# Long convolution and gated MLP in one kernel: matrices made ahead on GpSimd, conversions loaded from ScalarE's queue, tables copied

## The chip, the core and the metric

The kernel runs on one core of a Trainium2 chip. The core has TensorE (PE in the profile; its weight loads are PEld), VectorE (DVE), ScalarE (ACT), GpSimd (POOL) and SyncE (SP). Each takes its own instructions in a fixed order and waits at an instruction until what it needs is there. Transfers are issued by an engine's queue, in the kernel before by SP's alone, and run beside the engines. The metric is the device time of one execution in microseconds (us); of several executions the median counts.

## What is computed

```python
# attention block: batch 4, S = 12480, D = 128, filter order 64
h_filt = (np.maximum(pos_emb @ w1, 0.0) @ w2) * np.exp(-0.01 * pos)[:, None]
u = x * v
Uf = np.fft.rfft(u, n=2 * S, axis=1)
Hf = np.fft.rfft(h_filt, n=2 * S, axis=0)
y = np.fft.irfft(Uf * Hf[None], n=2 * S, axis=1)[:, :S, :]
x = (x * y).reshape(4 * S, D)
# mlp block: 128 -> 2048 -> 128
h = x @ w_in
out = ((h * np.cos(h)) @ w_out).astype(np.float32)
```

So a long convolution of `x*v` with a filter that is itself computed, a product with `x`, and an MLP with the activation h·cos(h). `moe_w_in` and `moe_w_out` arrive as float64.

## The kernel before

**The transform.** The convolution is done by a transform of length 2·96·120 that is split in two steps, N1 = 96 and N2 = 120, each a set of matrix products in float32. Rows of the sequence are taken in pairs (row and mirrored row), and their sums and differences are what the first step takes in. A batch entry goes through first step (`f1_units`, 64 units, one per pair of channels), second step (48 units, one per pair of frequencies k1), product with the filter's transform, and two inverse steps (`i1_units`, 64 units, and `i2_units`, 30 groups). The filter's transform is made once, together with the first batch entry's (`f2_both_units`), and stored in DRAM as `hd`; the matrices of the second step are stored as `wd`, and later batch entries load both.

**The order of the work.** It is written out by hand. `units` is a generator of the steps of one stage; the loops at the end of the kernel advance several such generators in turn, and every engine gets its instructions in the order in which Python emits them. Before 313 us the stages follow each other as this:

1. 0 to 26 us: the filter's MLP (`filter_turn`, `filter_hidden`). POOL computes angles for the sine tables (`Tables.sines`), ACT turns them into sines (`Tables.finish`, L227).
2. 26 to 52 us: `filter_out` (L371), 30 passes; between them `first_u` advances, the products and sums of x and v of the first batch entry (`u_multiply` L411, `u_sums` L421). Their loads (L394) come in through five places for pairs of rows, three pairs ahead. `ALONE` says from which pair on POOL takes a part.
3. 52 to 115 us: first step of the filter (L429; evicted by L448 and L450, four units of five by ACT, one by DVE). `first_u` goes on every second half-unit.
4. 115 to 156 us: first step of the first batch entry (L429, evicted by L441).
5. 156 to 256 us: second step of filter and batch entry together. For each pair `before` makes two matrices w (`make_w`: ACT writes a term into a bank of PSUM, L302, DVE adds the rest, L304) and stores them (L642); PE multiplies (L462, L465 for the filter, L135 for the batch entry); ACT copies the filter's part out as h (L653), which is stored (L655) and multiplied by DVE (L478) and summed by POOL (L485).
6. 256 to 312 us: first inverse step (L135 with `cs`), with `some_groups` making a part of the last step's tables beside it.

After that comes the main loop: the MLP's tiles, with the other convolution steps in between.

**The conversions.** `moe_w_in` and `moe_w_out` are turned from float64 words into float32 in 16 pieces of 128x256 during stages 3 and 4 (`convert_units`, `float32_store`): one load of 256 KB (L181), five DVE operations (L147 to L155), two on ACT (L160, L162), two on POOL (L163, L165), one store (L166). Loads run three pieces ahead through three buffers. One call of the generator is made every tenth half-unit from number 50 on; the first call only loads.

**The tables.** `inverse_tables` makes three tables with POOL and ACT, `cs` (120x2x120), `rows` (96x4x104) and `tw_t` (96x2x120). They lie in places that later stages overwrite, so they are stored in DRAM (L935) and loaded again: `cs` after stage 3/4's loop into a pool of its own (L953), the others after the second step (L965).

**Memory that is used twice.** The conversions' pool is given up when the last piece is done, and the pool of the second step (`both`: w, t, h) takes its place. Its first w is emitted eight half-units after the end of the conversions, still within the first step of the batch entry.

**PSUM.** Eight banks go round (`bank`). A half-filled order of evictions on ACT or DVE therefore stops PE after at most eight units.

Of the kernel before, what the change touches and what calls it, by code (L numbers as in the profile page):

```python
# [10 lines left out]
F32 = mybir.dt.float32  # L11
I32 = mybir.dt.int32
U32 = mybir.dt.uint32
AF = mybir.ActivationFunctionType
ALU = mybir.AluOpType
# [3 lines left out]
P = 128  # L19
# [15 lines left out]
def kernel(  # L35
# [46 lines left out]
    nc = tc.nc  # L82
# [4 lines left out]
    N1, N2 = 96, 120  # L87
# [3 lines left out]
    H = N2 // 2  # L91
# [18 lines left out]
    LAG = 7  # L110
    ALONE = 7
    WCOL = 256
# [28 lines left out]

    def float32_store(pool, dst, raw, factor):
        lo, hi = raw[:, :, 0], raw[:, :, 1]
# [14 lines left out]

        high = sig[:, :].bitcast(F32)
        nc.scalar.activation(high, sig[:, :], AF.Copy, scale=factor * 2.0 ** -20)  # L160
        low = pool.tile([P, WCOL], F32, name="low", bufs=1)
        nc.scalar.activation(low[:, :], lo, AF.Copy, scale=factor * 2.0 ** -52)  # L162
        nc.gpsimd.tensor_tensor(high, high, low[:, :], op=ALU.add)  # L163
        there = power[:, :].bitcast(F32)
        nc.gpsimd.tensor_tensor(there, high, there, op=ALU.mult)  # L165
        nc.sync.dma_start(dst, there)  # L166

# [7 lines left out]
    def convert_units(pool):  # L175

        raws = []
        for i, (dst, _, factor) in enumerate(pieces):
            while len(raws) < min(i + 3, len(pieces)):
                raws.append(pool.tile([P, WCOL, 2], U32, name="raw", bufs=3))  # L180
                nc.sync.dma_start(raws[-1][:, :, :], pieces[len(raws) - 1][1])  # L181
            yield
            float32_store(pool, dst, raws[i], factor)

# [69 lines left out]
    def inverse_tables(pool):  # L254

        t = Tables(pool, nc.gpsimd)
        part = t.whole([P, 1], [[1, 1]], channel_multiplier=1, name="part")
        part4 = t.whole([P, 1], [[1, 1]], base=1, channel_multiplier=4, name="part4")
        step = t.whole([P, P], [[1, P]], name="step")
        mid = t.whole([P, P], [[1, P]], base=-MID, name="mid")  # L260
        cs, (rows, tw_t) = third_table(pool), last_tables(pool)
        t.sines(step, part, N2, [(cs[:, 0, 0:H + 1], 1), (cs[:, 1, 0:H + 1], 0)],
                eighths=slice(0, H + 1, H))
        t.sines(step[:, 1:H], part, N2, [(cs[:, 0, H + 1:], 0), (cs[:, 1, H + 1:], 1)])
        t.sines(step, part4, 4 * N1, [(rows[:, i, :], q) for i, q in enumerate((0, 1, 2, 3))])
        t.sines(mid, part4, TURN, [(tw_t[:, 0, :], 1), (tw_t[:, 1, :], 0)],
                eighths=slice(H - 1, N2, H))
        return t, ((csd, cs), (rowsd, rows), (twd, tw_t))

# [12 lines left out]

    def third_table(pool):

        return pool.tile([N2, 2, N2], F32, name="cs")

# [23 lines left out]
    def make_w(w, k1, **how):  # L310


        turn(w, even[:, 0, :], even[:, 1, :], tw_w[:, 0, k1:k1 + 1], tw_w[:, 1, k1:k1 + 1],
             **how)

    def make_t(t, n2, copies=(), **how):
# [316 lines left out]
    def f2_both_units(bank):  # L633

        with tc.tile_pool(name="both", bufs=2) as pool:
            ws = {}

            def before(j):
                ws[j] = pool.tile([KE, 2, N2], F32, name="w")
                for i in range(2):  # L640
                    make_w(ws[j][:, i, :], 2 * j + i, half=bank)
                nc.sync.dma_start(wd[j, :, :, :], ws[j][:, :, :])  # L642

            def mm(j, ps, i):
                if i == 0:
                    ps = bank(), bank()
                for k in range(2):
                    f2_mm(ps[1 - i], ws[j], 2 * j, k, filt=i == 0)
                return ps

# [211 lines left out]
    with tc.manual_schedule():  # L862
        with tc.tile_pool(name="psum", bufs=8, space=PSUM) as psum, \
# [13 lines left out]
            with tc.tile_pool(name="layers", bufs=1, side="right") as pool:  # L877
# [26 lines left out]
                sines = forward_tables(pool)  # L904
                last_sines, made_tables = inverse_tables(between)
                peTs = {}
# [21 lines left out]
            for j in range(H // 2):  # L928
                filter_out(bank, aT, ftile, j, w2_sb)
                if j and j % 2 == 0:  # L930
                    last_sines.finish()
                for _ in range(1 + j % 2):
                    next(first_u)
            for kept, here in made_tables:
                nc.sync.dma_start(kept[:, :, :], here)  # L935
            keep.__exit__(None, None, None)
# [7 lines left out]
            with tc.tile_pool(name="convert", bufs=1) as pool:  # L944
                convert = convert_units(pool)
                for i, _ in enumerate(f1):
                    if i % 2 == 0:
                        next(first_u, None)
                    if i >= 50 and i % 10 == 0 and next(convert, True):
                        break  # L950
            lpool = ctx.enter_context(tc.tile_pool(name="late", bufs=1))
            cs = third_table(lpool)
            nc.sync.dma_start(cs[:, :, :], csd[:, :, :])  # L953
            f2 = f2_both_units(bank)
# [18 lines left out]
            with tc.tile_pool(name="ready", bufs=1) as pool:  # L973
                other = some_groups(pool)
                for i, _ in enumerate(i1_units(bank, lambda b: b % 8 == 3)):
                    if i % 4 == 0:
                        next(other, None)
# [110 lines left out]
```

## Time and profile before

| | us |
|---|---|
| three executions | 3684.23, 3684.69, 3687.74; median 3684.69 |
| profiled execution | 3686.0, its span 3684.2 |
| PE busy | 3609.0, 98% of the span |
| DVE, ACT, POOL busy | 2820.9, 2228.0, 2750.0 |
| granted clock of PE, mean | 0.997 |
| filter_out (L371), first to last | 25.9 to 51.6 |
| first step, filter (L429) | 52.5 to 114.7 |
| first step, batch entry (L429) | 114.8 to 156.3 |
| second step (L462, L465) | 156.5 to 251.9 |
| first inverse step | 256.2 to 310.4 |

How to read it: "busy" counts the time in which an engine had an instruction running. A row such as `L304 DVE ... w<-even,tw_w,ps 124x120 x2 [0.24 <-DMA wd<-w]` names the line, the engine, what is written from what, how many instructions were merged, and how long the engine stood idle before it and for whom. Records of PE matmuls are two for each matmul of float32. Instructions that issue transfers stand under their queue, SPq.

### The profile page before, as it was taken

What the parts mean: (1) busy time and instruction counts of PE and PEld (TensorE: products, weight loads), DVE (VectorE), ACT (ScalarE), POOL (GpSimd) and SP (SyncE); (2) the same over time, 40 slices, a digit from 0 to 9 for tenths busy, and PEclk for the clock granted to TensorE, in tenths of its full rate; (3) what the DMA queues carried; (4) which work ended last, traced back from release to release, by engine and by line L of the source; (5) the groups of instructions that cost most, each with busy time, mean ns of one, the idle gap of its engine ahead of it and who ended that gap; (6) DMA issues with size and microseconds to landing.
All of it is one profiled execution on the core that took longest, in us unless ns stands there. A gap on an engine that the chain in (4) does not pass through costs nothing.

```text
span 3684.2 us, 101739 instructions
## 1 busy us (share of the span) xinstructions
PE 3609.0 (98%) x40810; PEld 2552.8 (69%) x40810; DVE 2820.9 (77%) x5313; ACT 2228.0 (60%) x4474; POOL 2750.0 (75%) x3240
## 2 busy tenths in 40 slices
PE   7999999999999999999999999999999999999999
PEld 6777777766668776666667776766667786666666
DVE  6887886688887776688887777578887667777777
ACT  5666666665554556656555556665555446666666
POOL 7466996588874886588874887578884448878877
PEclk9999999999999999999999999999999999999999
DMA  6354541022213651022211662012220360000000
GB/s 183 113 174 124 160 144 31 18 70 70 70 48 85 171 157 29 18 70 67 74 41 32 174 167 75 13 53 70 71 69 16 88 170 22 19 23 20 19 25 14
DMA packets 226032, 281.78 MB, mean 76 GB/s; under 512 B 18883, under 2 KB 163067, under 8 KB 225435
## 3 DMA queue, kind: packets, MB, share of 16 engines
q1 hardware_dynamic: 225563, 275.29, 26.6%
q8 instruction: 324, 5.31, 0.6%
q14 instruction: 145, 1.19, 0.1%
HBM read 194.75 MB, written 80.46 MB: 75 GB/s over the span
## 4 chain that ended last, share of the span: by engine, by line
PE 83%; DVE 4%; POOL 2%; ACT 1%; issue 1%; DMA 0%; SPq 0%; ACTq 0%; POOLq 0%; DVEq 0%
PE ph L135 30%; PE cv L135 17%; PE accb L814 17%; PE acca L814 13%; PE cv L429 3%; PE cv L139 1%; DVE gt L789 1%; DVE gt L783 1%; PE ph L139 1%; ACT gt L782 1%; POOL ts L797 0%; POOL slots L421 0%; POOL ts L800 0%; ACT tile L845 0%; DVE xt L411 0%
## 5 line engine op out<-in xcount | busy, mean ns | idle before, releaser
L782 ACT ACTIVATE gt<-ph 128x512 int32<-128x512 f32 (+1 forms) x1380 | 823.1, 596 | 1147.0 <-PE ph L135 1087.4
L783 DVE SCALAR_TENSOR_TENSOR gt<-ph,gt 128x512 f32<-128x512 f32 (+1 forms) x1380 | 948.9, 688 | 717.1 <-ACT gt L782 714.1
L797 POOL TENSOR_TENSOR ts<-gt 128x512 f32<-128x512 f32 (+2 forms) x784 | 1006.5, 1284 | 582.5 <-PE accb L814 551.1
L135 PE MATMUL ph<-at,w_in_sb 128*64 128x512 f32 (+1 forms) x5520 | 1426.4, 592 | 13.5 <-ACT tile L845 6.5
L788 ACT ACTIVATE gt<-gt 128x512 f32<-128x512 f32 (+1 forms) x1568 | 971.8, 620 | 3.8 <-DVE gt L783 3.2
L789 DVE TENSOR_TENSOR gt<-ph,gt 128x512 f32<-128x512 f32 (+1 forms) x1380 | 936.0, 678 | 0.0
L814 PE MATMUL accb<-ts,w_out_sb 128*64 128x128 f32 (+2 forms) x9408 | 650.5, 272 | 0.0
L801 POOL TENSOR_TENSOR ts<-gt,ts 128x256 f32<-128x256 f32 (+2 forms) x784 | 575.6, 734 | 61.5
L800 POOL TENSOR_TENSOR ts<-ts,gt 128x256 f32<-128x256 f32 (+2 forms) x784 | 574.6, 733 | 61.5
L814 PEld LDWEIGHTS acca<-gt,w_out_sb 128*64 128x64 f32 x6272 | 398.5, 137 | 267.8 <-issue 231.5
L814 PEld LDWEIGHTS accb<-ts,w_out_sb 128*64 128x64 f32 x9408 | 544.2, 137 | 0.0
L814 PE MATMUL acca<-gt,w_out_sb 128*64 128x128 f32 (+2 forms) x6272 | 479.1, 272 | 0.0
L814 PEld LDWEIGHTS accb<-gt,w_out_sb 128*64 128x64 f32 x3136 | 225.1, 137 | 255.0 <-issue 198.7
L135 PEld LDWEIGHTS ph<-at,w_in_sb 128*64 128x64 f32 x5520 | 353.4, 137 | 33.3 <-ACT tile L845 14.7
L485 POOL TENSOR_TENSOR slots<-slots,t 120x256 f32<-120x256 f32 x383 | 281.1, 740 | 125.9 <-DVE t L484 68.4
L135 PEld LDWEIGHTS cv<-slots,tm 96*64 96x64 f32 (+1 forms) x3840 | 242.7, 126 | 120.2 <-issue 116.0
L814 PE MATMUL accb<-gt,w_out_sb 128*64 128x128 f32 (+1 forms) x3136 | 311.5, 273 | 4.8 <-DVE ot L835 3.2
L814 PE MATMUL acca<-ts,w_out_sb 128*64 128x128 f32 (+1 forms) x3136 | 308.4, 272 | 1.5 <-POOL ts L800 1.2
L135 PE MATMUL cv<-slots,tm 96*64 96x128 f32 (+1 forms) x3840 | 274.1, 285 | 3.9 <-DVE slots L507 3.4
L135 PEld LDWEIGHTS cv<-cs,slots 120*64 120x64 f32 (+1 forms) x3072 | 168.0, 125 | 61.1 <-issue 59.2
L814 PEld LDWEIGHTS acca<-ts,w_out_sb 128*64 128x64 f32 x3136 | 201.2, 137 | 3.0 <-POOL ts L800 2.7
L135 PE MATMUL cv<-slots,w 124*56 124x256 f32 (+1 forms) x1152 | 190.9, 406 | 1.9 <-ACT at L771 1.9
(136 smaller groups left out, 3742.9 us busy)
## 6 DMA issues: line engine op xcount, KB each, us to landing
h<-hd SPq DMA_DIRECT2D x144, 240.0 KB
tm<-td SPq DMA_DIRECT2D x96, 312.0 KB
xs<-in_x_dram SPq DMA_DIRECT2D x120, 208.0 KB
zd<-xs SPq DMA_DIRECT2D x119, 208.0 KB
tile<-zd SPq DMA_DIRECT2D x96, 256.0 KB
xt<-in_x_dram SPq DMA_DIRECT2D x90, 208.0 KB
vt<-in_v_dram SPq DMA_DIRECT2D x90, 208.0 KB
w<-wd SPq DMA_DIRECT2D x144, 116.2 KB
```

The lines of the kernel that those rows point to most:

```text
L135: nc.tensor.matmul(dst[lo:hi], left[:, lo:hi], right, start=start, stop=stop)
L139: nc.tensor.transpose(dst, src, ident[0:n, 0:n])
L429: nc.tensor.matmul(dst[lo:hi], u[:, b, lo:hi, i], c1[0:u.shape[0], r:r + 2, :].rearrange("p r k -> p (r k)"), start=True, stop=True)
L485: (engine if r else nc.gpsimd).tensor_tensor(y[:, r], y[:, r], t[:, r], op=op)
L782: nc.scalar.activation(turns, ph[:, 0:m], AF.Identity, bias=phase)
L783: nc.vector.scalar_tensor_tensor(out=part, in0=ph[:, 0:m], scalar=phase, in1=turns, op0=ALU.add, op1=ALU.subtract)
L788: nc.scalar.activation(part, part, AF.Sin, scale=scale)
L789: nc.vector.tensor_tensor(part, ph, part, op=ALU.mult)
L797: nc.gpsimd.tensor_tensor(ts[:, 0:2, 0:half], gt[:, :, half:2 * half], gt[:, 0, 0:2 * half].rearrange("p (h n) -> p h n", h=2), op=ALU.sub ...
L800: nc.gpsimd.tensor_tensor(t[2], t[1], b11, op=ALU.add)
L801: nc.gpsimd.tensor_tensor(t[3], b21, t[2], op=ALU.subtract)
L814: nc.tensor.matmul(acc[h * CB:(h + 1) * CB, place, 0:r], w_out_sb[:, pair, weight, :], right[:, h * r:(h + 1) * r], start=(pair == 0 and i ...
```

## The change

- *Tables.* The part of `cs` beyond its 61st column is no longer computed: it is copied from the other half when `cs` is stored. The third and fourth row table are the negated first and second, made by ACT. Six angle tables remain of ten; they are taken every third pass of `filter_out` instead of every second. All are stored by `store_tables` after the last pass. `cs` is loaded back into the memory of `even`, when the last matrix has been made from it.
- *Conversions.* The loads are issued from ACT's queue, at first two and then one piece ahead; the low part is written over its source; the store of a piece is issued a call later. Calls start at half-unit 40.
- *Matrices.* `early_matrices` makes the two matrices of every fourth pair (3, 7, ... 47: 24 matrices) on POOL during stages 3 and 4, from half-unit 30 on, every eighth, and stores them to `wd`. In the second step these pairs have no w; their matrices are loaded, each when the early pair before it has been multiplied.
- `ALONE` is 8 instead of 7; the side work of the first inverse step starts at half-unit 14 and comes twice in seven half-units instead of once in four.

```diff
-    ALONE = 7
+    ALONE = 8
+    EARLY = 4
@@ float32_store is now float32_made
-        high = sig[:, :].bitcast(F32)
+        high, low = sig[:, :].bitcast(F32), lo.bitcast(F32)
         nc.scalar.activation(high, sig[:, :], AF.Copy, scale=factor * 2.0 ** -20)
-        low = pool.tile([P, WCOL], F32, name="low", bufs=1)
-        nc.scalar.activation(low[:, :], lo, AF.Copy, scale=factor * 2.0 ** -52)
-        nc.gpsimd.tensor_tensor(high, high, low[:, :], op=ALU.add)
+        nc.scalar.activation(low, lo, AF.Copy, scale=factor * 2.0 ** -52)
+        nc.gpsimd.tensor_tensor(high, high, low, op=ALU.add)
...
-        nc.sync.dma_start(dst, there)
+        return lambda: nc.sync.dma_start(dst, there)
@@ convert_units
-        raws = []
+        raws, store = [], lambda: None
         for i, (dst, _, factor) in enumerate(pieces):
-            while len(raws) < min(i + 3, len(pieces)):
+            while len(raws) < min(i + 2, len(pieces)):
                 raws.append(pool.tile([P, WCOL, 2], U32, name="raw", bufs=3))
-                nc.sync.dma_start(raws[-1][:, :, :], pieces[len(raws) - 1][1])
+                nc.scalar.dma_start(raws[-1][:, :, :], pieces[len(raws) - 1][1])
+                if i:
+                    break
+            if i == 0:
+                yield
+            store()
+            store = float32_made(pool, dst, raws[i], factor)
             yield
-            float32_store(pool, dst, raws[i], factor)
+        store()
@@ inverse_tables
-        t.sines(step[:, 1:H], part, N2, [(cs[:, 0, H + 1:], 0), (cs[:, 1, H + 1:], 1)])
-        t.sines(step, part4, 4 * N1, [(rows[:, i, :], q) for i, q in enumerate((0, 1, 2, 3))])
+        t.sines(step, part4, 4 * N1, [(rows[:, i, :], i) for i in range(2)])
...
+        def store():
+            for i in range(2):
+                nc.scalar.activation(rows[:, 2 + i, :], rows[:, i, :], AF.Copy, scale=-1.0)
+                nc.sync.dma_start(csd[:, i, 0:H + 1], cs[:, i, 0:H + 1])
+                nc.sync.dma_start(csd[:, i, H + 1:], cs[:, 1 - i, 1:H])
+            for kept, made in ((rowsd, rows), (twd, tw_t)):
+                nc.sync.dma_start(kept[:, :, :], made)
@@ new
+    cs = even[0:N2]
+    def early_matrices(pool):
+        for j in range(EARLY - 1, N1 // 2, EARLY):
+            for i in range(2):
+                k1 = 2 * j + i
+                w = pool.tile([KE, N2], F32, name="made", bufs=3)
+                term = pool.tile([KE, N2], F32, name="term", bufs=1)
+                for h, dst in enumerate((w, term)):
+                    nc.gpsimd.tensor_scalar(out=dst[:, :], in0=even[:, h, :],
+                                            scalar1=tw_w[:, h, k1:k1 + 1], scalar2=None,
+                                            op0=ALU.mult)
+                nc.gpsimd.tensor_tensor(w[:, :], w[:, :], term[:, :], op=ALU.add)
+                yield
+                nc.sync.dma_start(wd[j, :, i, :], w[:, :])
@@ f2_both_units
             def before(j):
+                if j % EARLY == EARLY - 1:
+                    if j == EARLY - 1:
+                        load_early(j)
+                    return
...
+                if j == N1 // 2 - 2:
+                    nc.sync.dma_start(cs[:, :, :], csd[:, :, :])
+            def load_early(j):
+                if j < N1 // 2:
+                    ws[j] = pool.tile([KE, 2, N2], F32, name="early", bufs=1)
+                    nc.sync.dma_start(ws[j][:, :, :], wd[j, :, :, :])
...
+                if i and j % EARLY == EARLY - 1:
+                    load_early(j + EARLY)
@@ the loops
-                if j and j % 2 == 0:
+                if j and j % 3 == 0:
                     last_sines.finish()
...
-            for kept, here in made_tables:
-                nc.sync.dma_start(kept[:, :, :], here)
+            store_tables()
...
-                convert = convert_units(pool)
+                convert, matrices = convert_units(pool), early_matrices(pool)
                 for i, _ in enumerate(f1):
                     if i % 2 == 0:
                         next(first_u, None)
-                    if i >= 50 and i % 10 == 0 and next(convert, True):
+                    if i >= 24 and i % 8 == 6:
+                        next(matrices, None)
+                    if i >= 40 and i % 10 == 0 and next(convert, True):
                         break
-            lpool = ctx.enter_context(tc.tile_pool(name="late", bufs=1))
-            cs = third_table(lpool)
-            nc.sync.dma_start(cs[:, :, :], csd[:, :, :])
+                for _ in matrices:
+                    pass
...
-                    if i % 4 == 0:
+                    if i > 10 and i % 7 in (0, 3):
                         next(other, None)
```

More of the change, by code (lines that the diff above doesn't have):

```diff
@@ L139, in transpose, with float32_made @@
         nc.tensor.transpose(dst, src, ident[0:n, 0:n])
-    def float32_store(pool, dst, raw, factor):
+    def float32_made(pool, dst, raw, factor):
         lo, hi = raw[:, :, 0], raw[:, :, 1]
@@ L260, in inverse_tables @@
         mid = t.whole([P, P], [[1, P]], base=-MID, name="mid")
-        cs, (rows, tw_t) = third_table(pool), last_tables(pool)
+        cs = pool.tile([N2, 2, N2], F32, name="cs")
+        rows, tw_t = last_tables(pool)
         t.sines(step, part, N2, [(cs[:, 0, 0:H + 1], 1), (cs[:, 1, 0:H + 1], 0)],
                 eighths=slice(0, H + 1, H))
-        t.sines(step[:, 1:H], part, N2, [(cs[:, 0, H + 1:], 0), (cs[:, 1, H + 1:], 1)])
-        t.sines(step, part4, 4 * N1, [(rows[:, i, :], q) for i, q in enumerate((0, 1, 2, 3))])
+        t.sines(step, part4, 4 * N1, [(rows[:, i, :], i) for i in range(2)])
         t.sines(mid, part4, TURN, [(tw_t[:, 0, :], 1), (tw_t[:, 1, :], 0)],
                 eighths=slice(H - 1, N2, H))
-        return t, ((csd, cs), (rowsd, rows), (twd, tw_t))
+        def store():
[5 more added lines that the diff above has]
+                nc.sync.dma_start(kept[:, :, :], made)
+        return t, store
     class Between:
@@ L281, in tile @@
             return rows if len(shape) == 3 else rows[:, 0]
-    def third_table(pool):
-        return pool.tile([N2, 2, N2], F32, name="cs")
+    cs = even[0:N2]
     def last_tables(pool):
@@ L904 @@
                 sines = forward_tables(pool)
-                last_sines, made_tables = inverse_tables(between)
+                last_sines, store_tables = inverse_tables(between)
                 peTs = {}
```

## The prediction

> **What bounds the kernel now.** I read the page's engine rows first, then busy time by stretches of 10 us over the first 340 us, the waits of two stages, and the timeline at three places.
>
> ```profile
> PE 3609.0 (98%) x40810; PEld 2552.8 (69%) x40810; DVE 2820.9 (77%) x5313; ACT 2228.0 (60%) x4474; POOL 2750.0 (75%) x3240
> ```
>
> PE is busy for 98% of the span, so a gain can only come from where it isn't. The instructions that the diff touches all run before 313 us; after that the program is the same, and every microsecond won or lost before arrives at the end unchanged. The stretches (us from:to, length, busy us and instructions of PE, PEld, DVE, ACT, POOL, then clock, DMA share, GB/s):
>
> ```profile
> 60.00:70.00 10.00, 9.95 (x120) 9.65 (x120) 6.59 (x17) 5.93 (x22) 5.49 (x7) 1.00 0.70 195
> 70.00:80.00 10.00, 8.60 (x101) 7.96 (x102) 7.17 (x18) 3.25 (x12) 5.91 (x8) 1.00 0.73 212
> 80.00:90.00 10.00, 3.47 (x30) 2.49 (x28) 3.71 (x10) 2.49 (x10) 2.73 (x4) 0.79 0.79 223
> 90.00:100.00 10.00, 8.31 (x84) 6.37 (x82) 9.07 (x23) 4.97 (x20) 6.28 (x9) 0.84 0.47 126
> 100.00:110.00 10.00, 8.42 (x66) 6.01 (x64) 8.35 (x22) 5.17 (x22) 7.56 (x10) 0.68 0.28 75
> 170.00:180.00 10.00, 9.93 (x42) 6.75 (x41) 8.85 (x21) 5.91 (x15) 7.03 (x11) 1.00 0.60 181
> ```
>
> Two places are loose. The filter's first step (L429, 52.5 to 114.7) has 512 matmul records; at the 12 per us of the first row they need 42.7 us and take 62.2. The waits of 52 to 115 us (total, times, longest) say why:
>
> ```profile
> ACT sig L160 <- DVE sig L147: 21.6, 6, 10.5
> PE ps L429 <- ACT slots L450: 9.8, 3, 6.5
> DVE sig L147 <- DMA raw<-in_moe_w_in_dram: 7.0, 1, 7.0
> ```
>
> The first conversion's load arrives late, DVE stands on it, ACT behind DVE, PE behind both. The second place is the filter's second step (156.5 to 252), where PE looks full but its weight loads aren't (6.75 of 10). One pair of matrices there:
>
> ```profile
> 178.80 0.59 DVE L304 SCALAR_TENSOR_TENSOR w<-even,tw_w,ps 124x120 f32<-124x120 f32 x2 [0.24 <-DMA wd<-w]
> 179.31 0.69 DVE L478 TENSOR_TENSOR slots<-ps,h 120x512 f32<-120x512 f32 x1
> 179.42 0.24 SPq L642 DMA_DIRECT2D wd<-w  x1
> 179.91 0.68 DVE L478 TENSOR_TENSOR t<-ps,h 120x512 f32<-120x512 f32 x1
> 181.21 0.72 PEld L462 LDWEIGHTS ps<-ftile,w 124*120 124x120 f32 x4 [0.42 <-DVE w L304]
> ```
>
> The next w starts at 180.81, so the period is 2.02 us: 1.80 of DVE work and 0.22 for a buffer that its store still reads. PE waits 0.42 per pair for DVE: DVE is the bound.
>
> A third row fixes when that step may start:
>
> ```profile
> 146.02 0.59 DVE L304 SCALAR_TENSOR_TENSOR w<-even,tw_w,ps 124x120 f32<-124x120 f32 x2 [1.82 <-DMA woutd<-power]
> ```
>
> The step's first w reuses the conversions' memory, so it waits until they are over: GpSimd's (POOL's) last operation of them ended at 143.53, w started 2.5 us later. DVE stands meanwhile, and PE can go on only until its eight banks are used. From w there remain 0.6 us and 13 units of 0.65 (41.7 us over 64): 9.1 us, to 155.1; the step began at 156.5. PE has 1.4 us to spare.
>
> **The change part by part.** *Tables.* 18 POOL operations go (25.55 to 29.92 and 36.20 to 40.56): 8.7 us. DVE waited 9.5 us for POOL at 47, so products of x and v move forward by as much. Four Sin of 0.28 us go, two ScalarE negations come; three stores on SP become six (+0.6 us of issue), behind the negations at about 53 where SP now passes at 60. PE is at its full rate from 26 to 70, so this is worth nothing by itself. ALONE 8 moves one pair (0.73 and 0.97 us) from POOL to DVE, while DVE stood idle: nothing.
>
> *Loads.* 16 issues move from SP to ACT's queue, 0.37 us each (SP's row) or 0.93 (three took 2.78): 6 to 15 us of ACT, which is busy 2.5 to 6 of 10 there; hidden. What stands behind a held load on ACT are evictions, which PE waits for after eight banks, some 5 us. The first two are issued 10 half-units (of 0.37 us) ahead of their use, at about 67.4; landing took 3.0 us from the last of three issues and 5.8 from the first, I take 4.1: 71.5. From there DVE and ACT took 1.15 us and POOL's two operations 1.9 (86.18 to 89.26): the first conversion ends near 75, not 89. So the 7 us wait goes, and PE's idle time at 78 to 106 with it. It isn't won: what is late next is POOL.
>
> The Trainium skill (DMA: Bandwidth & Descriptors, Issuing engines are not separate DMA queues) says that transfers of all issuing engines interleave on the same DMA engines, so another queue saves issue time alone. By it the landing would be the longer 5.8 us and the sum 1.7 us later; no row here shows two queues at once.
>
> *Matrices.* 24 times two tensor_scalar and one tensor_tensor of 124x120 on POOL. Rows of that shape, of the first 50 us:
>
> ```profile
> L204 POOL TENSOR_SCALAR prod<-step,odd_p 124x120 f32<-124x120 f32 x1 | 0.6, 587 | 0.0
> L221 POOL TENSOR_TENSOR turned<-moved,turned 124x120 f32<-124x120 f32 x2 | 0.9, 439 | 0.2
> ```
>
> With the gaps of the timeline (0.69 from one to the next, 0.5 for the last) 1.88 us. Beside DVE work the same shapes took 0.96 and 0.82: 2.74 at worst. In the built order POOL still has, after the first conversion, 21 matrices (39.5), 15 conversions of two 0.73 us (22.5 with gaps) and 7 halves, 4 sums and a memset of x times v (9.9): 71.9 us without a pause, from 75 to 146.9. The last matrix's store must land too, 2.5 us: first w at 149.4, not 146.0. Less the 1.4 to spare, the second step starts 2.0 us later. With clean prices throughout (1.82 and 1.46) it is +0.1; with contended ones (2.2 and 1.87 each, 11 for the rest) POOL ends at 160.3 and it is +15.4. I stay near the clean end because of this pair:
>
> ```profile
> 119.63 0.73 POOL L163 TENSOR_TENSOR sig<-sig,low 128x256 f32<-128x256 f32 x1 [1.14 <-DVE power L153]
> 119.65 0.99 DVE L155 SCALAR_TENSOR_TENSOR power<-raw,power 128x256 uint32<-128x256 uint32 x1
> ```
>
> DVE's operation, 0.43 us alone, ended 0.28 after POOL's: they don't run at once, and DVE paid.
>
> The Trainium skill (SBUF — State Buffer, Who interferes with whom) names this: VectorE's tensor_scalar, or two inputs from SBUF, and GpSimd share a port pair as an exclusive lock, and who starts second waits. The trace agrees (0.99 against 0.43). Counted fully against POOL, that rule gives the contended end.
>
> SP's 24 matrix stores (0.24 each) are past SP's row loads, which run three pairs ahead; the loads no longer bind once POOL does.
>
> *Second step.* In 12 of 48 pairs ACT's two terms, DVE's w and its store go; a load of equal size comes, issued four pairs ahead (some 7 us against 3.4 of landing). Such a pair costs DVE 1.21, the others 1.80: 6.61 for four, PE's weight loads 4 times 1.61 = 6.44. One w in four still follows two pairs after the w whose buffer it takes (store issued 179.42, next use 3.4 later) with only 3.0 us of DVE work between: +0.4. So 7.05 for four instead of 8.08: 12 times 1.03 = 12.4 won, less 1.6 for the first such load, issued one pair ahead only: −10.8 (bounds −16, no wait; 0, below). The cosine table's reload lies under the last pairs; if it landed late, 2 to 3 us.
>
> *Third step* (256 to 310): PE's weight loads are full (10.0 of 10). Its side work starts 14 half-units later at a denser rhythm and reaches the same unit last (112): nothing.
>
> **Sum.** +2.0 − 10.8 = −8.8. The profiled execution took 3686.0 (span 3684.2 and 1.8 around it), 1.3 above the median: 3677.2 for it, 3675.9 against the median 3684.7. I say 3676. About 0.2%, 7.4 us, is what a measurement of this kernel can tell from no change: below 3677.3 or above 3692.1.
>
> **Rivals.** (a) *POOL's queue becomes the bound*: the contended prices, first w at 162.8 or later. For it: matrices are placed just where DVE's conversions run. Against: rows of 107 to 143, where POOL's operations stayed at 0.73. +15.4 − 10.8 = 3689; at 2.74 per matrix POOL ends near 171.5 and it is 3700. Slower than before from 2.30 us per matrix on (the rest as in the forecast: the queue then ends at 155.7). (b) *The second step is bound by transfers*: 356 KB per pair in 2.02 us are 176 GB/s, and the bytes stay. Then only the +2 is left, 3687. Against: DMA share 0.60 there, 0.70 at 195 GB/s earlier. (c) *No cost in the first step and no wait for stores*: −16 + 0.1, 3669. (d) *The loads don't come earlier*, ACT being held by what its issue waits for: first conversion at 89 as now, POOL's end 14 us later; 3690, priced like (a).
>
> **Numbers.** Forecast 0.50 (own range 3671 to 3682: 0.37 faster, 0.13 same); (a) with (d) 0.20 (slower 0.13, same 0.07); (b) 0.15, same; (c) 0.15, faster. Faster 0.52, same 0.35, slower 0.13. Range 3668 to 3691: it takes in (b), (c) and the near end of (a), and leaves out 0.15.
>
> **What will show it.** Right: wait for raw below 2 us; PE's idle time moves from 78–106 to just before the first w, at about 149; POOL busy nearly without a pause from 75 on, tensor_scalar of the matrices at 0.6 to 0.7; four pairs of the second step in 7.05 us, weight loads near 9 of 10. Wrong: POOL rows near 1 us, or pairs still at 2.02 us with waits for hd or wd.

## The result, and the profile after

The changed kernel is slower by 0.3%: 3697.4 us (median of 7 executions, 3696.0 to 3700.5) against 3686.5 (7, 3683.9 to 3690.3), a ratio of 1.0031 with a 95% interval of 1.0019 to 1.0042. The forecast was 3676 with a range up to 3691, and both its sign and its range were missed. The profiled execution took 3697.4, its span 3695.4; that of the kernel before 3686.0 and 3684.2.

The page's engine row of the changed kernel (busy us, share, instructions):

```profile
PE 3607.3 (98%) x40810; PEld 2558.0 (69%) x40810; DVE 2811.3 (76%) x5291; ACT 2215.1 (60%) x4448; POOL 2783.9 (75%) x3293
```

PE has the same work and the span is 11.2 us longer, so PE waited longer. The first start of each stage's matmuls, us, says where:

| | before | after | difference |
|---|---|---|---|
| first step, filter | 52.5 | 52.1 | -0.4 |
| first step, batch entry | 114.8 | 111.3 | -3.5 |
| second step | 156.5 | 164.2 | +7.7 |
| first inverse step | 256.2 | 267.4 | +11.2 |
| second inverse step | 312.2 | 324.3 | +12.1 |

Two places lost: the batch entry's part of the first step (52.9 us instead of 41.7) and the second step, which took 103.2 us to the start of the next instead of 99.7, where the forecast had counted on 10.8 us less. Busy time by stretches, the changed kernel (columns as in the prediction):

```profile
60.00:70.00 10.00, 10.00 (x126) 10.00 (x124) 6.15 (x16) 5.76 (x22) 8.68 (x13) 1.00 0.77 226
70.00:80.00 10.00, 7.11 (x85) 6.44 (x82) 8.99 (x21) 4.98 (x20) 9.08 (x13) 1.00 0.76 216
80.00:90.00 10.00, 7.28 (x66) 5.80 (x63) 5.22 (x13) 2.49 (x10) 9.60 (x14) 0.76 0.65 188
90.00:100.00 10.00, 5.77 (x56) 4.13 (x52) 6.43 (x17) 2.49 (x10) 9.68 (x14) 0.84 0.27 85
140.00:150.00 10.00, 6.18 (x77) 5.07 (x72) 2.02 (x5) 5.43 (x14) 9.43 (x17) 1.00 0.20 63
150.00:160.00 10.00, 6.87 (x62) 5.42 (x64) 2.43 (x6) 1.92 (x4) 0.44 (x1) 0.66 0.08 21
170.00:180.00 10.00, 7.25 (x26) 5.78 (x27) 4.58 (x10) 2.62 (x7) 3.92 (x6) 0.83 0.41 115
200.00:210.00 10.00, 9.69 (x44) 7.44 (x43) 8.62 (x19) 5.53 (x14) 7.08 (x10) 1.00 0.60 180
```

The fifth pair, POOL, is 8.7 to 9.7 of 10 from 60 on and stops at 150. PE still idles between 70 and 100, and again at 140 to 160. Who waited, changed kernel, 52 to 115 us (total, times, longest):

```profile
ACT sig L161 <- DVE sig L148: 22.3, 6, 6.1
DVE slots L449 <- POOL slots L439: 9.8, 6, 2.5
PE ps L457 <- ACT slots L478: 8.4, 3, 5.1
```

The 7 us wait for `raw` is gone, but DVE now waits for POOL's row products, which stand behind matrices in POOL's order; ACT waits for DVE, PE for ACT's evictions. The chain is the old one with another head. The end of POOL's queue, by the timeline:

```profile
150.00 0.44 POOL L340 TENSOR_TENSOR made<-made,term 124x120 f32<-124x120 f32 x1
152.73 0.59 DVE L317 SCALAR_TENSOR_TENSOR w<-even,tw_w,ps 124x120 f32<-124x120 f32 x2 [9.85 <-DMA wd<-made]
153.13 1.22 PE L457 MATMUL ps<-c,slots 104*64 104x192 f32 x6 [6.95 <-DVE w L317]
```

The first w of the second step came at 152.73 instead of 146.02, behind POOL's last matrix and its store, and PE, with all banks full, stood 6.95 us. POOL's rows from 55 to 152 us (busy, mean ns | idle before):

```profile
L337 POOL TENSOR_SCALAR made<-even,tw_w 124x120 f32<-124x120 f32 x24 | 17.7, 737 | 0.0
L337 POOL TENSOR_SCALAR term<-even,tw_w 124x120 f32<-124x120 f32 x24 | 16.7, 694 | 0.0
L163 POOL TENSOR_TENSOR sig<-sig,raw 128x256 f32<-128x256 f32 x16 | 12.3, 766 | 0.1
L340 POOL TENSOR_TENSOR made<-made,term 124x120 f32<-124x120 f32 x24 | 12.0, 498 | 2.0
```

A matrix costs 0.74 + 0.69 + 0.50 = 1.93 us, close to the 1.88 of the forecast. A stretch of the second step, where three pairs with w and one with an early tile (a pair whose matrices are loaded) take turns:

```profile
201.64 0.58 ACT L694 ACTIVATE h<-ps 120x512 f32<-120x512 f32 x1
203.23 0.24 SPq L674 DMA_DIRECT2D wd<-w  x1
203.56 0.84 SPq L696 DMA_DIRECT2D hd<-h  x2
206.38 0.60 ACT L694 ACTIVATE h<-ps 120x512 f32<-120x512 f32 x1 [2.06 <-DMA hd<-h]
207.01 0.69 DVE L506 TENSOR_TENSOR slots<-ps,h 120x512 f32<-120x512 f32 x1 [0.68 <-ACT h L694]
```

Where DVE had less to do, ACT waited 2.06 us for a buffer of h that its store still held, and DVE waited for ACT. Early loads were issued every 8.01 us (191.17 to 255.24, eight periods): four pairs took 8.01 us, against 4 times 2.02 before and 7.05 in the forecast. ACT waited 35.0 us for `hd<-h` in 24 waits; before it was 34.6 us in 43.

### The profile page after: what moved, and what is told of

Read it like the earlier page. It is cut to its first block, busy times and chain, and to the rows that moved or that the text cites. A ratio compares the mean times of both kernels' runs of the same rounds, so it can differ in the third digit from the quotient of the medians.

```text
span 3695.4 us, 101778 instructions
## 1 busy us (share of the span) xinstructions
PE 3607.3 (98%) x40810; PEld 2558.0 (69%) x40810; DVE 2811.3 (76%) x5291; ACT 2215.1 (60%) x4448; POOL 2783.9 (75%) x3293
## 4 chain that ended last, share of the span: by engine, by line
PE 84%; DVE 4%; POOL 1%; ACT 1%; issue 1%; DMA 0%; SPq 0%; ACTq 0%; POOLq 0%; DVEq 0%
PE ph L136 30%; PE cv L136 18%; PE accb L855 17%; PE acca L855 13%; PE cv L457 3%; PE cv L140 1%; DVE gt L830 1%; DVE gt L824 1%; PE ph L140 1%; ACT gt L823 1%; POOL ts L838 0%; POOL slots L449 0%; ACT tile L886 0%; DVE t L512 0%; POOL ts L841 0%
## 5 line engine op out<-in xcount | busy, mean ns | idle before, releaser
L855 PEld LDWEIGHTS acca<-gt,w_out_sb 128*64 128x64 f32 x6272 | 399.1, 137 | 267.4 <-issue 231.9
L136 PEld LDWEIGHTS ph<-at,w_in_sb 128*64 128x64 f32 x5520 | 353.4, 137 | 32.8 <-ACT tile L886 14.7
L136 PEld LDWEIGHTS cv<-slots,tm 96*40 96x40 f32 (+1 forms) x3840 | 243.3, 127 | 119.7 <-issue 115.0
L136 PEld LDWEIGHTS cv<-even,slots 120*33 120x33 f32 (+1 forms) x3072 | 168.0, 125 | 61.4 <-issue 58.8
L136 PE MATMUL cv<-slots,w 124*64 124x256 f32 (+1 forms) x1152 | 191.0, 406 | 1.9 <-ACT at L812 1.9
```

The costliest lines, as they stand in the source:

```text
L136: nc.tensor.matmul(dst[lo:hi], left[:, lo:hi], right, start=start, stop=stop)
L855: nc.tensor.matmul(acc[h * CB:(h + 1) * CB, place, 0:r], w_out_sb[:, pair, weight, :], right[:, h * r:(h + 1) * r], start=(pair == 0 and i ...
```

## The experiments

Three questions: are the matrices what made the first step late, or the loads (theory Q, GpSimd's queue, against L); what are tables and loads worth alone; and what holds the second step. Kernels without matrices have `EARLY = 1000`. Ratios are to the kernel before on the same chip. A stage's start is read from one trace and holds to about 2.5 us only: among traces whose program is the same up to there, the second step began at 156.5 to 158.9 (the kernel before and its two runs with a cut store), at 164.2 to 166.2 (five runs with all matrices) and at 147.1 to 149.9 (five with tables and loads, conversions from half-unit 40, no matrices).

**Without matrices, two ways.**

```diff
-    EARLY = 4
+    EARLY = 1000
```

> The changed kernel with no matrix made ahead: ScalarE and VectorE make all 96 again, and there are no early loads; loads, later stores and tables stay as changed. Theory Q (GpSimd's queue): the 24 matrices, 46.4 us of GpSimd, are what made the first step late. Without them GpSimd's conversions end near 122 us instead of 147, the first w of the second step no longer waits (9.85 us now), the first step of the batch entry ends near 145 instead of 163.9, the second step keeps the 2.02 us a pair it had before (95.6 us in all): 3697 - 19 - 2 = about 3676, faster than the kernel before. Theory L (loads): what made the first step late are the raw loads on ScalarE's queue, with the evictions behind them: the first step still ends near 160, and the time is 3692 to 3697.

Measured: 3679.6 us, ratio 0.9981 (0.9972 to 0.9990). The first w no longer kept PE waiting, the second step began at 148.7. In this kernel, and in the one with a third buffer for w further below, the last pair's w is made from memory that `cs` is already loaded into: its values are not the reference's, and it waits for that load. The run was repeated with the reload behind that w:

```diff
-                if j == N1 // 2 - 2:
+                if j == N1 // 2 - 1:
                     nc.sync.dma_start(cs[:, :, :], csd[:, :, :])
```

> The changed kernel with no matrix made ahead, as before, and the third step's table reloaded one pair later, behind the last w that is made from the memory it overwrites (in the first run without matrices the last pair's w was made from the overwritten tables, and waited for that load). Theory Q: tables, loads and later stores are worth some 8 us by themselves and the matrices lose more than that: 3677 (3675 to 3679). If the gain of the first run came from the overwritten pair: 3683 to 3687.

Measured: 3676.1, ratio 0.9973 (0.9963 to 0.9983); second step from 149.9, first inverse step from 249.6. Theory Q holds, L falls: the matrices, with their loads in the second step, cost 21 us, 14.3 of them before the second step begins.

**The loads undone, the matrices kept.** Loads on SP's queue, three pieces ahead, from half-unit 50, each store at once.

> The changed kernel with the conversions' loads back on SyncE's queue, three pieces ahead, first step as in the kernel before, and each store right behind its piece; the matrices stay. Theory Q: GpSimd's queue starts with the first conversion near 87 instead of 74, still has the matrices, and ends 8 to 13 us later than 150: the first w near 160 to 165, time 3705 to 3710. Theory L: the first step is rid of what made it late and ends near 156 as before; with the second step's 98 us the time is 3688 to 3691.

Measured: 3702.2, ratio 1.0040 (1.0027 to 1.0054), the first w at 157.8 and the second step from 170.0. The direction is that of Q, the size less: the first w came 5.0 us and the second step 5.8 us later than in the changed kernel, instead of 8 to 13, and the time is below the expected 3705 to 3710.

**Half as many matrices** (`EARLY = 8`; w's store behind h's, as in the run `after_swap` below).

> The run before with every eighth pair made ahead instead of every fourth: 12 matrices, 23 us of GpSimd instead of 46. Theory Q with T: GpSimd's queue ends near 130 to 135 instead of 150, the first w no longer keeps TensorE waiting, the second step starts at 148 to 150 as without matrices, and eight pairs take some 15 us instead of 16.1, less 3 us for the first early load: 3673 to 3676. Theory Q with R: the first step is the same and the second gains nothing: 3679 to 3681. If half the matrices already delay the first w, it starts above 155 and the time is above 3681.

Measured: 3694.0, ratio 1.0022 (1.0013 to 1.0031); the second step from 154.3, neither 148 to 150 nor above 155. POOL's queue was over well before, and PE did not wait for the first w; but the filter's part of the first step ended at 112.6, as with all 24 (111.3 to 113.5), instead of 105.4 to 108.2 without any: the calls come at the same rhythm, so all 12 fall into the filter's part, and each matrix in the queue also delays the row products behind it. In the second step the late stores of w cost 5.21 us at the second pair, which has nothing to do with the matrices, and eight pairs took 16.8 us, more than either theory had; the time is 13 us above what Q allowed, and the second step has most of that.

**Tables alone, the queue, and a later start.** First the tables (with `ALONE` and the third step's rhythm), the conversions as in the kernel before:

> The run with tables and loads, with the conversions' loads on SyncE's queue, three ahead, stores at once and first step as in the kernel before: what is left of the change are the tables (and one pair moved to VectorE). By the prediction's step the tables are worth nothing: 3685 to 3687, the second step starting at 156. Theory W: the row products that move forward give VectorE and GpSimd room before the conversions, and part of the 10 us comes from here: 3679 to 3683.

Measured: 3677.8, ratio 0.9977 (0.9968 to 0.9986). This was worth nothing in the forecast and is nearly all that the change had to give (`ALONE` and the rhythm were not tried without the tables). The second step began at 152.1 instead of 156.5, and the 4.4 us arrived unchanged at the first inverse step (251.7) and the second (307.7). A stretch where a part of them comes from, first before, then with the tables alone:

```profile
50.00:60.00 10.00, 7.57 (x74) 6.41 (x72) 8.42 (x17) 5.22 (x19) 7.05 (x9) 1.00 0.70 198
```

```profile
50.00:60.00 10.00, 9.45 (x104) 8.72 (x104) 5.82 (x15) 6.61 (x24) 4.99 (x7) 1.00 0.61 162
```

In the kernel before, PE waited there for DVE, which had row products to catch up on that POOL's tables had held back (waits of 50 to 66 us):

```profile
PE ps L429 <- DVE slots L450: 1.9, 1, 1.9
```

PE is busy for 1.9 us more there, and for 1.6 us more between 66 and 110 (34.4 instead of 32.8 of 44).

Then ACT's queue against SP's, with everything else of the loads kept (`nc.scalar.dma_start(raws[-1]...)` becomes `nc.sync.dma_start`):

> The run with tables and loads, with the raw loads issued by SyncE again, but two ahead, from the earlier half-unit and with the stores one piece later. If the queue is what counts (loads held on SyncE behind row loads that wait for their buffers), the first conversion is late again, and the time is 3682 to 3687; if the earlier issue and the later stores are what count, 3675 to 3678.

Measured: 3681.6, ratio 0.9986 (0.9977 to 0.9995), just below the one expectation (3682 to 3687) and 4 us above the other. The queue seems to count: DVE waits 5.4 us for `raw` again, in two waits, against 2.7 in one; but the intervals of the two ratios (this one and 0.9963 to 0.9983) still meet. Against the tables alone (3677.8), the loads on ACT's queue were worth 1.7 us and a second step that began 2.2 us earlier, both no more than these medians and single traces can tell from nothing.

Then later conversions:

```diff
-                    if i >= 40 and i % 10 == 0 and next(convert, True):
+                    if i >= 60 and i % 10 == 0 and next(convert, True):
```

> The run with tables and loads, with the conversions begun 20 half-units later (60 instead of 40). Theory D: what is left of TensorE's idle time at 70 to 100 us (some 6 us and a lower clock after it) comes from row loads and raw loads sharing the transfers (215 to 224 GB/s there) and from conversions standing between the row products on VectorE and GpSimd; later conversions give the rows way: the filter's part ends 3 to 5 us earlier, the conversions end near 139, just before the first w is needed, and the time is 3671 to 3674. If the rows alone fill that stretch, or the conversions then end too late: 3676 to 3680.

Measured: 3671.3, ratio 0.9959 (0.9946 to 0.9971); the second step from 143.6. Its stretches:

```profile
70.00:80.00 10.00, 10.00 (x128) 10.00 (x126) 6.19 (x17) 4.51 (x18) 5.06 (x6) 1.00 0.76 216
80.00:90.00 10.00, 7.16 (x71) 5.68 (x69) 7.90 (x20) 4.45 (x19) 6.74 (x10) 0.88 0.66 195
```

Between 66 and 110 us PE idles 2.9 us instead of 5.9 (start at 40) and 11.2 (before): conversions that start among the row products hold those up, and with them PE. Whether by their operations on DVE and POOL or by their loads, this run doesn't part.

> The run with tables and loads, with the conversions begun at half-unit 70 (40 in the change, 60 in the best run so far: 3671.3, conversions over at 137 us, second step from 143.6). Theory D, as before: another 1 to 2 us of TensorE's idle time between 66 and 110 us go (2.9 us are left at 60), but the conversions now end near 140 and the first w comes near 142 to 143, 7 or 8 us before TensorE needs it, so it no longer has its 9 us: 3670 to 3673, the same as at 60. If the last conversions decide: 3674 to 3678.

Measured: 3670.4, ratio 0.9952 (0.9938 to 0.9965), second step from 144.1: the same as at 60. PE idles 3.2 us between 66 and 110, so the further 1 to 2 us that were expected there didn't come.

**The second step: buffers, order, queue.** A third buffer for w, then the store of w behind that of the h made before it, then both, and h's store from ACT's queue:

```diff
-                ws[j] = pool.tile([KE, 2, N2], F32, name="w")
+                ws[j] = pool.tile([KE, 2, N2], F32, name="w", bufs=3)
```

> As the run without matrices, and the second step's w has three buffers instead of two (the room of the early tile). Theory T (turnaround): the pace of the second step is set by how long a stored buffer stays taken; VectorE's 0.22 us wait for the store of w goes, a pair takes 1.80 to 1.88 us instead of 2.02, and the run is 6 to 10 us below the one without matrices. Theory R (rate): 356 KB a pair at some 180 GB/s set the pace; then the wait moves from w to h, the period stays at 2.0 and the times are within 2 us of each other.

> The changed kernel, matrices and all, with the store of w issued behind the store of the h made before it. Theory T: four pairs take 7.0 to 7.2 us instead of 7.8 and the wait of h's making for its store (35 us in 24 waits) falls below 10: 3688 to 3690. Theory R: 7.7 to 7.9 for four, 3695 to 3699.

> As the run with tables and loads alone, with w in three buffers and the store of w issued behind the store of the h that is made before it, so that on SyncE's queue h's store no longer stands behind VectorE's w (1.75 us from h's end to its store in the trace of before). Theory T (turnaround: 3 buffers of h in 0.6 + 1.75 + 0.4 + 3.3 = 6.05 us, 2 of w in 4.03, both 2.02 a pair): both cycles are loosened, a pair takes 1.80 to 1.86 us, what VectorE's own work needs, and the time is 3667 to 3670. Theory R (rate): 356 KB a pair at 176 to 183 GB/s stay at 1.95 to 2.02 a pair: 3675 to 3679.

> The changed kernel with the second step's store of h issued by ScalarE, which makes h, instead of by SyncE, where it stands behind the store of w. In the trace of the changed kernel h of the third pair of four was ready at 202.2 and stored at 203.6. Theory T (turnaround of h's three buffers): four pairs take 7.1 to 7.4 us instead of 7.8, and the time is 5 to 8 us below the changed kernel's 3697. Theory R (rate, 183 GB/s for any order): four pairs stay at 7.7 to 7.9 and the time at 3696 to 3699.

Measured, in the same order:

- third buffer for w: 3680.5 (the run without matrices 3679.6), 2.02 us a pair;
- w's store behind h's, all matrices: 3700.0, ratio 1.0039 (1.0025 to 1.0052), 8.06 us for four pairs;
- both, no matrices: 3677.4 (against 3676.1), 2.02 us a pair;
- h's store from ACT's queue, all matrices: 3707.3, ratio 1.0055 (1.0042 to 1.0069), 9.26 us for four pairs.

None moved the pace down. Whatever was loosened, the wait moved: in the third, h's store was issued at once, and its buffer came back later.

```profile
205.71 0.32 SPq L701 DMA_DIRECT2D hd<-h  x1
211.19 0.60 ACT L699 ACTIVATE h<-ps 120x512 f32<-120x512 f32 x1 [0.78 <-DMA hd<-h]
```

That is 5.2 us from the end of the issue to the next use; before it was 3.3 us after an issue 1.75 us later. Theory T (turnaround) falls; R (transfers) stays for now. With ACT's queue the wait for w's store rose from 4.3 to 20.9 us in all, and two queues together moved less (155 GB/s at 240 to 250 us, 186 in the changed kernel). That the second queue brought no more agrees with the Trainium skill (DMA: Bandwidth & Descriptors, Issuing engines are not separate DMA queues), by which transfers of all issuing engines share the same transfer engines.

**Half of h.** Only the first half of each h is stored; later loads read it twice. Of these two runs there is one execution each, and only the pace of the second step is read.

> The changed kernel, storing only the first half of every h in the second step (120 KB instead of 240); where the later stages load h, they load that half twice, in two transfers, so that the output of later batches is not the reference's and only the second step of the first batch is to be read here. Theory R (transfer rate, some 182 GB/s): four pairs move 945 KB instead of 1425 and need 5.3 us of transfers, so VectorE's work and its waits set the pace: 6.7 to 7.1 us for four instead of 7.8, as the prediction had it. Theory T' (a landing of 3 to 5 us whatever the size, by the number of transfers): 7.6 to 7.9.

Measured: four pairs in 7.32 us instead of 8.01, between the two expectations. The same with the better order and three buffers:

> The run with w in three buffers and its store behind that of h (no matrices made ahead, 2.02 us a pair, every buffer returned only 5.2 us after its store was issued), storing only the first half of every h in the second step; where the later stages load h they load that half twice, so that the output of later batches is not the reference's and only the first batch's second step is to be read. Theory R (bytes): 236 KB a pair need 1.3 us at 182 GB/s, the stores return in 3 us or less, nothing waits for them any more, and VectorE's own work sets the pace: 1.80 to 1.86 us a pair, no wait for hd or wd to speak of. Theory T' (a return that does not depend on size): stores still return after 5 us and a pair takes 1.95 to 2.02.

Measured: 1.76 us a pair (the mean of 23 periods from 192.1 us on; the same count gives 2.05 for the kernel before). These means contain a few pauses; from one w to the next without a pause it is 1.71 us, and 2.02 in the kernel before. DVE, the third pair, then has no pause:

```profile
210.00:220.00 10.00, 10.00 (x71) 9.13 (x70) 10.00 (x25) 6.94 (x17) 8.27 (x13) 1.00 0.47 143
```

So the transfers hold the second step. But 182 GB/s is not what the transfer engines can move (256 GB/s at 250 to 260 us of the run with 112 and 12 rows below), and their mean share is 0.60. A quarter-microsecond view of one pair of the kernel before (the last two columns are the DMA share and GB/s):

```profile
181.50:181.75 0.25, 0.25 (x3) 0.18 (x2) 0.25 (x1) 0.25 (x1) 0.25 (x1) 1.00 1.00 302
182.00:182.25 0.25, 0.25 (x3) 0.21 (x2) 0.25 (x2) 0.22 (x2) 0.14 (x1) 1.00 0.43 159
182.25:182.50 0.25, 0.25 (x3) 0.22 (x2) 0.25 (x1) 0.25 (x2) 0.00 (x0) 1.00 0.26 89
```

All transfer engines are busy for a moment, and then 0.26 of them, 4.2 of 16.

**Number of engines (theory F).** w's store covers 124 rows. It is cut in two, unevenly and, as a control, in halves:

```diff
-                nc.sync.dma_start(wd[j, :, :, :], ws[j][:, :, :])
+                for rows_ in (slice(0, 112), slice(112, KE)):     # control: 62
+                    nc.sync.dma_start(wd[j, rows_, :, :], ws[j][rows_, :, :])
```

> The kernel before with one edit: the second step's store of w is issued as two transfers, rows 0 to 111 and rows 112 to 123, instead of one of 124 rows. Theory F (four engines): in each pair the DMA share falls to 0.26, about 4 of 16 engines, while w is stored; those four carry 31 rows of 960 bytes and 8 of 2 KB a pair, 46 KB in 2.02 us, the others 16 KB. Split, w's rows spread over more engines, the stores return earlier and VectorE's work sets the pace: 1.80 to 1.86 us a pair, share without dips to 0.26, no more than 5 us of waits for hd and wd, 3677 to 3679. The Trainium skill (DMA: Bandwidth & Descriptors, Why a DMA increments its semaphore by 16 and not by 1) gives the rule behind it: a transfer runs on the largest number of engines up to 16 that divides its outermost size, so 124 rows on 4, 112 on 16, 12 on 12 and h's 120 on 15. Theory R (bytes at 182 GB/s): the bytes are the same, the pace stays at 2.02 and the time at 3685 to 3688.

> The kernel before with the second step's store of w issued as two transfers of 62 rows each, a control for the split in 112 and 12. Theory F (number of engines): no size above 2 and up to 16 divides 62, so each half runs on two engines and nothing is won; a pair takes 2.02 us or more, 3686 or slower. Theory S (two smaller transfers return sooner, whatever they run on): 1.80 to 1.90 us a pair and 3674 to 3679, as with 112 and 12.

Measured, on the kernel before: 112 and 12 rows 3675.7, ratio 0.9971 (0.9959 to 0.9982), 1.84 us a pair; 62 and 62 rows 3747.9, ratio 1.0161 (1.0144 to 1.0178), 3.42 us a pair (both over 23 periods; without pauses 1.70 and 3.40). The stretch with 112 and 12, against 0.60 and 181 GB/s in the prediction's row of the same time:

```profile
170.00:180.00 10.00, 10.00 (x48) 8.26 (x47) 10.00 (x24) 6.40 (x17) 8.38 (x12) 1.00 0.73 207
```

And two quarter-microseconds with 62 and 62:

```profile
201.75:202.00 0.25, 0.25 (x3) 0.18 (x2) 0.25 (x2) 0.25 (x2) 0.00 (x0) 1.00 0.15 46
202.25:202.50 0.25, 0.25 (x3) 0.21 (x2) 0.25 (x1) 0.25 (x1) 0.00 (x0) 1.00 0.13 42
```

0.13 is two engines of sixteen. Theory F holds: two smaller transfers alone make it much worse, and what counts is how many engines share the rows. Theory R, a fixed rate for the bytes, falls with it: the same bytes moved at 207 GB/s. One sign was not met: with 112 and 12 rows ACT still waited 18.9 us for `hd<-h` between 165 and 235 us, where 5 were expected; but in the stretch shown DVE has no pause, and it sets the pace. The bytes agree too, if the transfers run on the numbers of engines in the expectation: the busiest engine carries 31 rows of 960 bytes and 8 of 2 KB, 46 KB in 2.02 us or 22.8 KB per us; with 62 rows, both halves on the same two engines, 76 KB in 3.40 us, 22.3; with half of h 38 KB, which at 22.8 needs 1.67 us, less than DVE's 1.71. The views show no engine by itself, so the count is read from the shares. The packet records that each trace keeps (start, duration and size of every packet of a transfer) bear it out: counted every 0.02 us over the second step, packets of 960 bytes, the rows of w, are most often four at a time in the kernel before and two with 62 and 62 rows, and they reach 16 and more with 112 and 12. The Trainium skill (DMA: Bandwidth & Descriptors, Why a DMA increments its semaphore by 16 and not by 1) states the rule that a transfer uses the largest number of engines up to 16 that divides its outermost size; the shares of 0.26 and 0.13 agree with its 4 for 124 and 2 for 62.

**The cut in the changed kernel, and in the best one.**

> The changed kernel, matrices and all, with the stores of w and the loads of the early pairs in the second step split in rows 0 to 111 and 112 to 123. Theory F: four pairs take 6.7 to 7.1 us instead of 8.0, as the prediction had counted, and the first early load lands sooner: 11 to 15 us less, 3682 to 3686, the same as or a little below the kernel before; the first step is as late as it was. Theory R: four pairs stay at 8.0, 3696 to 3699.

> Tables and loads without matrices, conversions from half-unit 60 (3671.3), and the store of w split in rows 0 to 111 and 112 to 123. Theory F: another 8 to 11 us: 3660 to 3663. Theory R: 3670 to 3672.

Measured: 3680.5, ratio 0.9983 (0.9974 to 0.9992), with the second step as late as ever (165.7) and four pairs in 7.02 us (early loads from 174.50 to 244.66, ten periods). That is 1.5 us less than expected at best. And 3660.0, ratio 0.9927 (0.9915 to 0.9940): tables, loads from ACT's queue begun at half-unit 60, no matrices, w's store cut. It is 27 us or 0.7% below the kernel before, and below the changed kernel too.

## Why the prediction was wrong, step by step

*Tables, "worth nothing by itself".* Wrong by its reading. "PE is at its full rate from 26 to 70" doesn't hold for 50 to 60, where the view read first has 7.57 of 10; the row was neither shown nor weighed. DVE's row products, put off by POOL's tables, stood before evictions there. Measured 4.4 us by the trace, 9 by the medians; against the other two traces with the first step of the kernel before it would be 5.9 and 6.8.

*Loads.* The mechanism held: first conversion's last operation at 73.94 to 74.71 (forecast 75, before 89), no wait for `raw`. "It isn't won: what is late next is POOL" held as well. That PE's idle time "moves to just before the first w" is half right: it came there (6.95 us), and 11.3 us remained between 66 and 110, for the forecast let POOL's backlog count only at its end, while every product in the queue is somebody's input.

*Matrices.* The price was right (1.93 against 1.88), the end of the queue 3.5 us late (150.4 against 146.9), the first w 3.3 us (152.7 against 149.4). From w to the second step it then took 11.4 us instead of 9.1: after the idle time the granted clock was 0.50 until 156.8 us, 0.66 over the stretch of 150 to 160. So +7.7 instead of +2.0. Rival (a) gave such a time, by contended prices that didn't come; its price of 2.30 us per matrix was not needed. (The rows of 0.96 and 0.82 us behind its 2.74 are of tiles of 124x96, not of "the same shapes".)

*Second step, -10.8.* This is the step that failed, by 14 us: the inverse step began 3.5 us later still. "PE waits 0.42 per pair for DVE: DVE is the bound" took an engine's 1.80 us of work for the pace of 2.02, and its 0.22 us wait for `wd<-w` for a local loss. A row beside those shown said that ACT waited too, for `hd<-h`, and it did so in 42 of the 48 pairs, 33.2 us in all:

```profile
179.39 0.60 ACT L653 ACTIVATE h<-ps 120x512 f32<-120x512 f32 x1 [0.73 <-DMA hd<-h]
```

What the runs showed in its place: the transfers set the pace, because w's 124 rows and their share of h load four of the 16 transfer engines. Less work for DVE doesn't shorten that (a pair without w loads its matrices, on as many rows), and four pairs stayed at 8.01 us. Rival (b), at 0.15, was right that the transfers bind, and wrong that the bytes do; it was put back for the mean share of 0.60, which hides four busy engines under twelve idle ones. With w's store and the early loads cut, four pairs take 7.02 us against the forecast's 7.05. In part that is luck: there a pair with w takes 1.70 to 1.75 us, not 1.80, and the wait that remains, some 0.5 us in four pairs, is DVE's for ACT's h, not for w's store. The first early load kept PE's weight loads waiting for 3.5 us instead of 1.6, and with the cut 1.66.

*Third step, "nothing".* +0.9 us: 55.4 us instead of 54.5, begun at a lower clock (0.86 at 270 to 280) after a longer pause.

*The sum.* -8.8 was +2.0 - 10.8; measured +7.7, +3.5 and +0.9 are 12.1 at the second inverse step. No rival joined a late first step to an unmoved second one, and so the range ended at 3691.

## What to carry to other kernels

When two engines wait in each period for stores to return, the transfers set the pace, and an engine's own work is no price for what its relief will win; look at the DMA share in slices shorter than the period, because a share that falls to a quarter says more than its mean. The outermost size of a transfer decides here how many engines carry it: 124 rows cost 2.05 us a pair, the same rows as 112 and 12 1.84, as 62 and 62 3.42. And work given to an engine "off the path" isn't only due at its end: in a queue without gaps it delays every operation behind it, so price it by the first one that somebody waits for.

## What was not expected of the hardware

- With one transfer of 124 rows and 116 KB in each pair, three quarters of the transfer engines stood idle for a part of the pair (share 0.26), with two of 62 rows seven eighths (0.13); the same bytes as 112 and 12 rows raised the stretch from 181 to 207 GB/s.
- Buffers came back later when their stores were issued earlier: 5.2 us instead of 3.3, at the same 2.02 us a pair. Until the pace of the transfers was known, that looked like a slow return.
- After 7 us of idle time PE worked at a granted clock of 0.50 for 3.7 us, until 156.8 us, and work that was estimated at 9.1 us took 11.4.
